# Four small VectorE steps of a query softmax rewritten for GpSimd, the turned halves in a slot of their own, and a new table of order offsets

## The chip, the cores and the metric

The kernel runs on one core of a Trainium2 chip. The metric is the device time of one execution in microseconds (us). Three runs of the kernel before the change took 1722.93, 1723.33 and 1721.21 us, a median of 1722.93. The execution whose profile is read below took 1722.68 us; its span from the first to the last instruction is 1721.0 us, so 1.7 us lie outside the span.

Five engines work side by side: PE (TensorE, matrix products), DVE (VectorE), ACT (ScalarE), POOL (GpSimd) and SP (SyncE, which here only issues DMAs). Each engine takes its instructions in the order in which the program lists them and waits at each for what that instruction needs.

## What is computed

Two attention blocks on 2048 tokens of width 1024 with 32 heads of 32, their outputs side by side. The change touches block B, a linear attention whose feature map is a pair of softmaxes:

```python
def _B_ref(x, wqkv, w_phi, wo):
    q, k, v = ...                                      # x @ wqkv, by heads
    pq = jnp.einsum("bhsd,hdf->bhsf", q, w_phi)
    pk = jnp.einsum("bhsd,hdf->bhsf", k, w_phi)
    phi_q = jnp.concatenate([_softmax(pq, axis=-1), _softmax(-pq, axis=-1)], axis=-1)
    phi_k = jnp.concatenate([_softmax(pk, axis=-1), _softmax(-pk, axis=-1)], axis=-1)
    kv = jnp.einsum("bhsf,bhsd->bhfd", phi_k, v)
    z  = jnp.einsum("bhsf->bhf", phi_k)
    num = jnp.einsum("bhqf,bhfd->bhqd", phi_q, kv)
    den = jnp.einsum("bhqf,bhf->bhq", phi_q, z)[..., None] + 1e-6
    o = num / den
    return ... @ wo
```

Block A is a causal attention over four segments with a running memory, and ends in its own product with an output matrix.

## The kernel before

**Stages.** Times are from the trace. From 0 to about 850 us run 32 units of block A (attention, with B's weights folded and B's tokens prepared between them). From about 850 to 927 us B's first values follow, up to 1189 us the keys and remaining values of B in eight pairs of 128-token tiles, from 1189 to about 1573 us B's queries (the *query stage*), and from 1561 us to the end the output product of block A.

**Products.** Numbers are kept as two float16 halves (a high part and the rest), so a product is three matrix instructions. The large products go by a Strassen scheme over a pair of token tiles: seven half-size products into three PSUM banks X, Y and Z (`strassen`, products at L610), four results out.

**The query stage** runs over 16 token tiles `c`. For each even `c` one Strassen product of 84 instructions gives four results, one for each tile of the pair and each half `hb` of the heads. `expo` takes each result: per-head maximum and minimum (L1264), the two differences into the tile `e` (L1266, L1268), four exponentials (ACT, L1271), the sums of both softmaxes (L1274) and their reciprocals `r` (L1277). Then for each tile and `hb`, a *unit* (32 in all): GpSimd multiplies `e` by the key sums `zb` in two parts (L1579), VectorE sums each part (`dn`, L1582), then four small VectorE instructions make the common factor: `dn*r` (L1585), both halves of it added with 1e-6 (L1587), its reciprocal (L1589), and `r` times that reciprocal times 2^14 (L1590). GpSimd multiplies `e` by `r` (L1592). ACT writes the high half of the result as float16 (L1601), VectorE the rest (L1603), both into a tile `eh`. SP turns `eh` with a transposing DMA into `pt` (L1606). PE multiplies `pt` by the key-value sums `kls` (24 instructions, L1615), ACT and VectorE write both halves of that to `ot` (L1619, L1621), and `project` multiplies `ot` by B's output matrix (48 instructions for a tile, L396) and stores it.

**Buffers.** A buffer with a tag is a ring: a new one takes the place of the one as many back as the ring has places, and its first writer waits for all uses of that older one. `e` and `eh` share the ring "e" of five. For a pair of tiles the program asks for four `e`, then four `eh`, then the next pair's four `e`. So the `eh` of the second unit takes the place of the first `e`, and the first `e` of the next pair that of the fourth `e` of this pair. Slots S0 to S15 are single buffers of [128, 2, 4, 512] float16. The seven forms of the query weights lie in the slots listed in `VS` (S0, S1, S2, S3, S9, S11, S15).

**A's output weights** are also made in the query stage, on ACT and GpSimd (`weights`, in tiles 5, 7, 9, 11): of their seven forms, B11, B21 and T1 are written straight into slots S8, S13 and S12, the other four go over buffers `cs` to DRAM (`wo_d`) and are loaded at tile 14 (L1568) into the first slots of the query weights.

**The order.** The program doesn't fix the order of instructions by hand. Each operation is given to `Graph.op` with an engine, a planned duration, a priority (the stage's number) and what it reads and writes. `Graph.run` walks through a planned time and at each step lets the ready operation with the lowest priority go next on its engine; `lat` and `kb` tell it how long a DMA takes to land. That list is what each engine then runs in order. Operations with the same priority in a row are a *job*; the table `MOVES` adds an offset to the priority of one engine's part of one job. Job numbers 20 to 235 belong to block A and the values, 238 to 284 to the keys, 285 to 390 to the query stage.

Of the kernel before, what the change touches and what calls it, by code (L numbers as in the profile page):

```python
# [18 lines left out]
S = 2048  # L19
# [22 lines left out]
VS = (0, 1, 2, 3, 9, 11, 15)  # L42
# [12 lines left out]
         ((3, 0, "subtract"), 3, 2), ((2, 3, "subtract"), 2, 6))  # L55
EUP = 2.0 ** 15
MOVES = {
# [6 lines left out]
    "DVE": {  # L64
# [4 lines left out]
    "ACT": {  # L69
# [3 lines left out]
    "POOL": {  # L73
        59: 0.5, 67: 5.5, 70: -0.5, 93: -6, 141: 5, 154: -8, 173: 3, 199: 12, 202: -3, 211: -16.5, 234: -5.5, 238: -29.5,
        250: -2, 252: 1.5, 257: 0.5, 312: -11.5, 326: -7},
    "SP": {
        88: 5, 89: 2.5, 107: -2.5, 131: 3, 134: 21.5, 183: 8, 184: -7, 223: 6.5, 226: -9, 238: -37},
}


# [197 lines left out]
SP, PE, ACT, DVE, POOL = "SP", "PE", "ACT", "DVE", "POOL"  # L278
# [3 lines left out]
def tile_kernel(ctx: ExitStack, tc: tile.TileContext, ax, aw, awv, awo, beta, bx, bwqk, bwv, bphi, bwo, out):  # L282
    nc = tc.nc
# [5 lines left out]
    dram = ctx.enter_context(tc.tile_pool(name="scratch", bufs=1, space=DRAM))  # L289
    oa_d = dram.tile([NT, 128, NG, 128], F32, name="oa_d")  # L290
    wf_d = dram.tile([3, 7, 128, 2, 4, 512], F16, name="wf_d")
    xf_d = dram.tile([NT // 2, 128, 7, 2, 4, 128], F16, name="xf_d")
    wo_d = dram.tile([4, 128, 2, 4, 512], F16, name="wo_d")
    bo_d = dram.tile([2, 2, 128, 2, 4, 512], F16, name="bo_d")
    wa_d = dram.tile([NG, 128, 2, 2, NC, 128], F16, name="wa_d")
    wva_d = dram.tile([4, 128, 2, NC, 256], F16, name="wva_d")
# [56 lines left out]
    for t in vfb:  # L353
        nc.gpsimd.memset(t[:, :, 128:132], 1.0)

    G = Graph(pools)
    op = G.op
# [5 lines left out]
       w=[gates], prio=0.2, lat=2.0, kb=16)  # L363
# [919 lines left out]
    def ev(e):  # L1283
        return e().rearrange("p h s d -> p (h s d)")
# [86 lines left out]
    for at_, p in enumerate(SEQ):  # L1371
        P = PB + 2 * at_
# [126 lines left out]
    for n in range(2):  # L1499
        for q in range(2):  # L1500
            op(SP, 0.6, lambda n=n, q=q: nc.sync.dma_start(bo[n][q](), bo_d[n, q]), r=[(bob, (n, q))],
               w=[lanes[q]] + [(bo[n][q], (a, i)) for a in range(2) for i in range(4)], prio=P + 1, lat=1.0, kb=1024)
    wform = {}
    ast = G.buf("b", [128, 16], F32, "ast", 1)

    def blocks(j, prio):
# [15 lines left out]
            op(DVE, 0.1, lambda: nc.vector.tensor_tensor(wsc[:, 2, 1, 0:1], wsc[:, 2, 0, 0:1], osc2[:, 0, 0:1], op=OP.mult),  # L1522
               r=[(wscs, (2, 0)), (oscs, 0)], w=[(wscs, (2, 1))], prio=prio)

    SECOND, wob = ("T2", "T3", "B22", "T4"), G.fixed(wo_d)

    def weights(j, prio):

# [17 lines left out]
    for c in range(NT):  # L1546
# [9 lines left out]
                x = x1 if c == 0 else xkept(c // 2 + 1, XS, P)  # L1556
        ot = G.buf("b", [128, 2112], F16, "ot", 4)
        if c == 2:
            for f, i in (("B11", 8), ("B21", 13), ("T1", 12)):
                wform[f] = G.buf("slot", [128, 2, 4, 512], F16, f"S{i}")  # L1560
        if c in (1, 2, 3, 4):
            sizes_out(c - 1, P + 0.5)
# [1 line left out]
            weights((c - 5) // 2, P + 0.5)  # L1564
        if c == 14:
            for i, f in enumerate(SECOND):
                wform[f] = G.buf("slot", [128, 2, 4, 512], F16, f"S{i}")
                op(SP, 0.6, lambda i=i, f=f: nc.sync.dma_start(wform[f](), wo_d[i]), r=[(wob, i)],  # L1568
                   w=[(wform[f], (a, n)) for a in range(2) for n in range(4)], prio=P + 0.5, lat=1.0, kb=1024)

# [3 lines left out]
        for hb in range(2):  # L1574
            e, r = er[c % 2, hb]
            dn = G.buf("b", [128, 16, 2], F32, "dn", 2)
            for a in range(2):
                h0 = 16 * hb + 8 * a
                op(POOL, 1.35, lambda a=a, h0=h0, e=e: nc.gpsimd.tensor_tensor(  # L1579
                    e()[:, 8 * a:8 * a + 8], e()[:, 8 * a:8 * a + 8], zv()[:, h0:h0 + 8], op=OP.mult),  # L1580
                   r=[zb, r], w=[(e, ("x", a))], prio=P)
                op(DVE, 0.66, lambda a=a, e=e, dn=dn: nc.vector.tensor_reduce(  # L1582
                    dn()[:, 8 * a:8 * a + 8], e()[:, 8 * a:8 * a + 8], axis=AX.X, op=OP.add), r=[(e, ("x", a))], w=[(dn, a)], prio=P)
            d1 = G.buf("b", [128, 16], F32, "d1", 2)
            op(DVE, 0.1, lambda dn=dn, r=r: nc.vector.tensor_tensor(dn(), dn(), r(), op=OP.mult),  # L1585
               r=[dn, r], w=[dn], prio=P)
            op(DVE, 0.1, lambda dn=dn, d1=d1: nc.vector.scalar_tensor_tensor(  # L1587
                d1(), dn()[:, :, 0], 1e-6, dn()[:, :, 1], op0=OP.add, op1=OP.add), r=[dn], w=[d1], prio=P)
            op(DVE, 0.15, lambda d1=d1: nc.vector.reciprocal(d1(), d1()), r=[d1], w=[d1], prio=P)  # L1589
            op(DVE, 0.1, lambda d1=d1, r=r: nc.vector.scalar_tensor_tensor(  # L1590
                r(), r(), 2.0 ** 14, d1()[:, :, None].to_broadcast([128, 16, 2]), op0=OP.mult, op1=OP.mult), r=[d1, r], w=[r], prio=P)
            op(POOL, 1.95, lambda e=e, r=r: nc.gpsimd.tensor_tensor(e(), e(), bc32(r), op=OP.mult),  # L1592
               r=[e, r], w=[e], prio=P)
            pt = G.buf("b", [128, 2, 8, 128], F16, "pt", 3)
            eh = G.buf("b", [128, 16, 2, 32], F32, "e", 5)

            def hv(eh=eh):
                return eh().rearrange("p h s d -> p (h s d)").bitcast(F16).rearrange("p (a n) -> p a n", a=2)

            for q in range(2):  # L1600
                op(ACT, 0.53, lambda q=q, e=e, hv=hv: nc.scalar.activation(  # L1601
                    hv()[:, 0, 512 * q:512 * q + 512], ev(e)[:, 512 * q:512 * q + 512], AF.Copy), r=[e], w=[(eh, (0, q))], prio=P)
                op(DVE, 0.7, lambda q=q, e=e, hv=hv: nc.vector.tensor_tensor(  # L1603
                    hv()[:, 1, 512 * q:512 * q + 512], ev(e)[:, 512 * q:512 * q + 512], hv()[:, 0, 512 * q:512 * q + 512], op=OP.subtract),
                   r=[e, (eh, (0, q))], w=[(eh, (1, q))], prio=P, port=True)
            op(SP, 0.6, lambda pt=pt, hv=hv: nc.sync.dma_start_transpose(  # L1606
                pt().rearrange("p a g t -> p (a g) t"), hv().rearrange("p a n -> p (a n)")),
               r=[(eh, (a, q)) for a in range(2) for q in range(2)], w=[pt], prio=P, lat=2.0, kb=512)
            pn = bank("pv", [128, 4, 128])

            def f(pn=pn, pt=pt, hb=hb):
                for g in range(4):
                    for a, b in ((0, 0), (0, 1), (1, 0)):
                        for k in range(2):
                            nc.tensor.matmul(pn()[64 * k:64 * k + 64, g, :], kls()[:, a, 8 * hb + 2 * g + k, :], pt()[:, b, 2 * g + k, :],  # L1615
                                             start=(a + b == 0), stop=(a == 1), skip_group_check=True)

            op(PE, 0.85, f, r=[(kls, (0, hb)), (kls, (1, hb)), pt], w=[pn], prio=P)
            op(ACT, 0.55, lambda pn=pn, hb=hb, otv=otv: nc.scalar.activation(  # L1619
                otv()[:, 0, 4 * hb:4 * hb + 4, :], pn(), AF.Copy, scale=2.0 ** -15), r=[pn], w=[(ot, (0, hb))], prio=P)  # L1620
            op(DVE, 0.62, lambda pn=pn, hb=hb, otv=otv: nc.vector.scalar_tensor_tensor(  # L1621
                otv()[:, 1, 4 * hb:4 * hb + 4, :], pn(), 2.0 ** -15, otv()[:, 0, 4 * hb:4 * hb + 4, :], op0=OP.mult, op1=OP.subtract),
               r=[pn, (ot, (0, hb))], w=[(ot, (1, hb))], prio=P)
# [117 lines left out]
```

## Time and profile before

| | us |
|---|---|
| median of three runs | 1722.93 |
| the profiled execution | 1722.68 |
| its span | 1721.0 |
| PE busy | 1670.3 (97% of the span) |
| DVE busy | 1408.9 (82%) |
| ACT busy | 1159.6 (67%) |
| POOL busy | 955.2 (56%) |
| mean granted TensorE clock | 0.992 |

How to read it: the profile's page gives busy time by engine and by slices of the span; groups of instructions by line, with busy time, mean duration and the idle time of the engine just before them together with what ended that idle time; and the chain of waits that ended last. "x" is a count. A matrix instruction's duration includes its way through the array, and the next one starts before it ends: busy PE is not PE at its peak, so the prediction counts instructions and multiplies by their spacing. PEclk is the granted share of TensorE's clock. An instruction that is held inside its engine counts as busy, with a longer duration.

### The profile page before, as it was taken

The numbers are of one execution on the slowest core, as the hardware profiler recorded it, in microseconds if no ns is written. First come the engines' busy times: TensorE is split into PE (matmuls) and PEld (weight loads), VectorE is DVE, ScalarE is ACT, GpSimd is POOL, SyncE is SP. The second block draws the span as 40 slices with busy tenths as digits, with TensorE's granted clock in tenths as the row PEclk, the third lists the DMA queues.
The fourth block names the chain that finished last, engine by engine and source line by source line (L and its number), as shares of the span: only waits on it lengthen the run. The fifth ranks groups of instructions, "written<-read, shape, count | busy, mean of one in ns | idle before, by whom it ended". The sixth has DMA issues, their size and how long they took to land.

```text
span 1721.0 us, 38652 instructions
## 1 busy us (share of the span) xinstructions
PE 1670.3 (97%) x14408; PEld 1002.9 (58%) x14408; DVE 1408.9 (82%) x3269; ACT 1159.6 (67%) x2131; POOL 955.2 (56%) x1184
## 2 busy tenths in 40 slices
PE   8999999999999999999999999999799899999999
PEld 6667677676776776677755545455344444444444
DVE  6999999899998767797885889778999999987441
ACT  8788999888888978678854676665445554345331
POOL 3346588653668775756742678645656767440000
PEclk9999999999999999999999999999989999999999
DMA  6556456666666573764467464566456565646311
GB/s 211 162 167 185 155 186 190 216 182 184 196 188 204 148 217 94 203 192 115 150 189 258 148 215 135 177 220 251 156 125 149 127 175 128 196 107 198 121 67 61
DMA packets 260699, 290.37 MB, mean 169 GB/s; under 512 B 138784, under 2 KB 191776, under 8 KB 253984
## 3 DMA queue, kind: packets, MB, share of 16 engines
q1 hardware_dynamic: 260512, 287.91, 55.7%
q8 instruction: 113, 1.85, 0.5%
q14 instruction: 74, 0.61, 0.1%
HBM read 160.12 MB, written 85.00 MB: 142 GB/s over the span
## 4 chain that ended last, share of the span: by engine, by line
PE 45%; DVE 15%; DMA 2%; ACT 2%; issue 1%; POOL 1%; SPq 0%; DVEq 0%; ACTq 0%; POOLq 0%
PE proj L610 14%; PE proj L396 8%; PE proj L1669 5%; PE s L610 3%; PE misc L396 3%; DVE e L1603 3%; PE s L1669 2%; DMA pt<-e 2%; PE misc L610 2%; DVE mx L1264 2%; DVE r L1274 1%; DVE dn L1582 1%; PE pv L1009 1%; PE s L973 1%; PE misc L1669 1%
## 5 line engine op out<-in xcount | busy, mean ns | idle before, releaser
L396 PE MATMUL proj<-S,S 128*128 128x128 f16 (+1 forms) x3072 | 504.6, 300 | 4.8 <-DVE S L431 1.8
L396 PEld LDWEIGHTS <-S 128*128 128x128 f16 x4608 | 329.7, 98 | 150.7 <-issue 9.3
L610 PE MATMUL proj<-S,S 128*128 128x512 f16 x1584 | 368.4, 381 | 8.3 <-ACT cs L616 6.1
L610 PEld LDWEIGHTS <-S 128*128 128x128 f16 x2016 | 191.9, 98 | 226.1 <-issue 12.8
L986 POOL TENSOR_SCALAR_AFFINE_SELECT ph<-ph 128x256 f16<-128x256 f16 (+1 forms) x448 | 194.3, 456 | 165.5 <-DVE ph L980 147.9
L878 DVE CUSTOM_DVE_ANT_0 s<-s,causal 128x256 f32<-128x256 f32 (+3 forms) x512 | 242.9, 508 | 14.1 <-PE s L872 10.8
L980 DVE SCALAR_TENSOR_TENSOR ph<-s,ph 128x512 f16<-128x512 f32 x320 | 211.0, 684 | 51.6 <-ACT ph L979 50.2
L979 ACT ACTIVATE ph<-s 128x512 f16<-128x512 f32 x320 | 191.5, 659 | 0.8
L396 PE MATMUL misc<-S,ot 128*128 128x512 f16 x768 | 172.5, 382 | 1.1 <-ACT ot L1619 1.1
L1271 ACT ACTIVATE e<-e,sk 128x256 f32<-128x256 f32 x256 | 113.8, 497 | 55.3 <-DVE e L1268 46.1
L396 PEld LDWEIGHTS <-ot 128*128 128x128 f16 x768 | 74.2, 98 | 90.8 <-issue 2.2
L1579 POOL TENSOR_TENSOR e<-e,zb 128x512 f32<-128x512 f32 x64 | 86.1, 1369 | 56.5 <-DVE r L1274 45.4
L973 PE MATMUL s<-S 104*128 104x512 f16 (+3 forms) x512 | 114.7, 299 | 0.9 <-DVE mu L951 0.5
L872 PE MATMUL s<-S 96*128 96x512 f16 (+3 forms) x512 | 113.2, 299 | 0.8 <-DVE mt L878 0.4
L977 ACT ACTIVATE s<-s,os 128x512 f32<-128x512 f32 x160 | 106.2, 714 | 9.5 <-PE s L973 6.8
L977 ACT ACTIVATE s<-s,bd 128x512 f32<-128x512 f32 x160 | 106.8, 712 | 5.5 <-PE s L973 4.8
L396 PE MATMUL proj<-wv,S 128*128 128x128 f16 x1536 | 104.9, 219 | 0.1
L1601 ACT ACTIVATE e<-e 128x512 f16<-128x512 f32 x64 | 37.3, 622 | 97.0 <-POOL e L1592 47.5
L1009 PEld LDWEIGHTS <-ph 128*128 128x128 f16 x2560 | 87.3, 96 | 17.7 <-issue 1.4
L1009 PE MATMUL pv<-vl,ph 128*128 128x66 f16 (+1 forms) x2560 | 92.2, 184 | 0.8 <-DVE h L826 0.3
L1274 DVE TENSOR_REDUCE r<-e 128x32 f32<-128x1024 f32 x64 | 76.6, 1207 | 12.5 <-ACT e L1271 12.4
L1592 POOL TENSOR_TENSOR e<-e,r 128x1024 f32<-128x1024 f32 x32 | 64.8, 2029 | 39.6 <-DVE r L1590 35.8
(342 smaller groups left out, 3355.2 us busy)
## 6 DMA issues: line engine op xcount, KB each, us to landing
S<-xf_d SPq DMA_DIRECT2D x126, 256.0 KB
S<-h SPq DMA_DIRECT2D x192, 128.0 KB
S<-wf_d SPq DMA_DIRECT2D x21, 1024.0 KB
st<-bwqk SPq DMA_DIRECT2D x64, 256.0 KB
out<-os SPq DMA_DIRECT2D x40, 256.0 KB
S<-aw SPq DMA_DIRECT2D x16, 512.0 KB
wa_d<-S SPq DMA_DIRECT2D x16, 512.0 KB
wf_d<-fo SPq DMA_DIRECT2D x32, 256.0 KB
```

What stands on the lines that cost most here:

```text
L396: op(PE, dur, lambda c=c, a=a, b=b, lv=lv, rv=rv: nc.tensor.matmul(pv(), lv(), rv(), start=(c == 0 and a + b == 0), stop=(c == n - 1 and a ...
L610: op(PE, 0.215, lambda n=n, a=a, b=b, lv=lv, rv=rv: nc.tensor.matmul(ps(), lv(), rv(), start=(start and n == 0 and a + b == 0), stop=(n == ...
L872: nc.tensor.matmul(ps()[:, o:o + 128 * i + 128], st()[0:96, 0, h, 128 * i:128 * i + 128], st()[0:96, 1, h, 0:128 * i + 128], start=True, s ...
L878: dve(0.12 + 0.00113 * n, lambda h=h, i=i, o=o, n=n: nc.vector.tensor_tensor_reduce(ps()[:, o:o + n], ps()[:, o:o + n], causal[:, 512 - n: ...
L973: nc.tensor.matmul(ps()[:, o:o + n], st()[0:104, 1, h, 128 * j:128 * j + 128], st()[0:104, 0, h, 128 * j:512], start=True, stop=True)
L977: act(0.59, lambda: nc.scalar.activation(ps(), ps(), AF.Exp, bias=0.0, scale=bdv()[:, 3, i2, 0:1]), r=[(bd, i2)], w=[ps])
L979: act(0.5, lambda: nc.scalar.activation(ph()[:, 0], ps(), AF.Copy, scale=2.0 ** 14), r=[ps], w=[(ph, 0)])
L980: dve(0.6, lambda: nc.vector.scalar_tensor_tensor(ph()[:, 1], ps(), 2.0 ** 14, ph()[:, 0], op0=OP.mult, op1=OP.subtract), r=[ps, (ph, 0)], ...
L986: nc.gpsimd.affine_select(pd, pd, pattern=[[0, n], [1, 128]], compare_op=OP.is_ge, fill=0.0, base=0, channel_multiplier=-1)
L1009: nc.tensor.matmul(ps()[:, i, n0:n1], ph()[:, a, o:o + 128], vl()[:, j, h, n0:n1], start=(i == 0 and a == 0), stop=(j == min(i, 2)), skip_ ...
L1271: op(ACT, 0.41, lambda i=i: nc.scalar.activation(e()[:, 4 * i:4 * i + 4], e()[:, 4 * i:4 * i + 4], AF.Exp, bias=0.0, scale=sk()[:, i:i + 1 ...
L1669: op(PE, 0.215, lambda n=n, a=a, b=b: nc.tensor.matmul(ps(), v(a)[:, n, :], wform[w]()[:, b, n, :], start=(start and n == 0 and a + b == 0 ...
```

## The change

1. In each unit of the query stage `dn*r`, the scaling and the product of `r` with the reciprocal move to GpSimd as three instructions (planned at 0.25 us each). The sum of the two halves of `dn` becomes a reduction on VectorE; 1e-6 and the factor 2^14 go into the GpSimd instruction behind it (as 2^-14 ahead of the reciprocal). VectorE keeps the reduction and the reciprocal.
2. `eh` leaves the ring "e". One buffer in slot S13, [128, 2, 2048] float16, holds the halves of both `hb`; each `hb` has its own part of it.
3. Form B21 of A's output weights leaves S13: its halves go over `cs` to DRAM too (`wo_d` has five places), and it is loaded at tile 14. The five loaded forms go into the first five slots of `VS`: S0, S1, S2, S3, S9.
4. The transposing DMA is planned with 2.9 us on SP instead of 0.6, a landing time of 1.2 instead of 2.0 and 64 KB instead of 512 of DMA flow.
5. `MOVES` is replaced as a whole, with entries for all stages (jobs 20 to 363 before, 43 to 384 now).

```diff
 MOVES = {
+    "DVE": {
+        43: -3, 44: -1, 70: 2.5, 85: -19, 88: -3.5, 93: -7.5, 101: -3.5, 103: 7, 106: -22.5, 109: 2.5, 113: -3.5, 114: -9.5,
...
+        222: -14, 229: -1, 238: -62.5, 243: -1.5, 250: -19, 296: -0.5, 307: 2, 308: -40.5, 312: -15.5, 317: -2, 318: -15.5,
+        332: 5, 338: -11.5, 350: -2.5, 358: -1.5, 370: 3, 381: -13.5, 387: -7.5},
...
     "PE": {
-        20: -6.5, 22: -12.5, 76: -7, 79: -15.5, 83: -4, 96: -5, 101: 2, 102: 4, 104: 2, 107: 5.5, 108: 15.5, 113: 1.5,
...
     "SP": {
-        88: 5, 89: 2.5, 107: -2.5, 131: 3, 134: 21.5, 183: 8, 184: -7, 223: 6.5, 226: -9, 238: -37},
+        88: 7, 89: 7, 151: 6.5, 167: 6, 169: 2.5, 199: 9.5, 217: -5, 250: -6, 363: 4.5},
 }
...
-    wo_d = dram.tile([4, 128, 2, 4, 512], F16, name="wo_d")
+    wo_d = dram.tile([5, 128, 2, 4, 512], F16, name="wo_d")
...
+    eh = G.buf("slot", [128, 2, 2048], F16, "S13")
...
-    SECOND, wob = ("T2", "T3", "B22", "T4"), G.fixed(wo_d)
+    SECOND, wob = ("B21", "T2", "T3", "B22", "T4"), G.fixed(wo_d)
...
-            for f, i in (("B11", 8), ("B21", 13), ("T1", 12)):
+            for f, i in (("B11", 8), ("T1", 12)):
...
-                wform[f] = G.buf("slot", [128, 2, 4, 512], F16, f"S{i}")
+                wform[f] = G.buf("slot", [128, 2, 4, 512], F16, f"S{VS[i]}")
...
-            op(DVE, 0.1, lambda dn=dn, r=r: nc.vector.tensor_tensor(dn(), dn(), r(), op=OP.mult),
+            op(POOL, 0.25, lambda dn=dn, r=r: nc.gpsimd.tensor_tensor(dn(), dn(), r(), op=OP.mult),
                r=[dn, r], w=[dn], prio=P)
-            op(DVE, 0.1, lambda dn=dn, d1=d1: nc.vector.scalar_tensor_tensor(
-                d1(), dn()[:, :, 0], 1e-6, dn()[:, :, 1], op0=OP.add, op1=OP.add), r=[dn], w=[d1], prio=P)
+            op(DVE, 0.12, lambda dn=dn, d1=d1: nc.vector.tensor_reduce(d1(), dn(), axis=AX.X, op=OP.add), r=[dn], w=[d1], prio=P)
+            op(POOL, 0.25, lambda d1=d1: nc.gpsimd.tensor_scalar(d1(), d1(), 1e-6, 2.0 ** -14, op0=OP.add, op1=OP.mult), r=[d1], w=[d1], prio=P)
             op(DVE, 0.15, lambda d1=d1: nc.vector.reciprocal(d1(), d1()), r=[d1], w=[d1], prio=P)
-            op(DVE, 0.1, lambda d1=d1, r=r: nc.vector.scalar_tensor_tensor(
-                r(), r(), 2.0 ** 14, d1()[:, :, None].to_broadcast([128, 16, 2]), op0=OP.mult, op1=OP.mult), r=[d1, r], w=[r], prio=P)
+            op(POOL, 0.25, lambda d1=d1, r=r: nc.gpsimd.tensor_tensor(
+                r(), r(), d1()[:, :, None].to_broadcast([128, 16, 2]), op=OP.mult), r=[d1, r], w=[r], prio=P)
...
-            eh = G.buf("b", [128, 16, 2, 32], F32, "e", 5)
-
-            def hv(eh=eh):
-                return eh().rearrange("p h s d -> p (h s d)").bitcast(F16).rearrange("p (a n) -> p a n", a=2)
+            def hv(hb=hb):
+                return eh()[:, hb].rearrange("p (a n) -> p a n", a=2)
...
-            op(SP, 0.6, lambda pt=pt, hv=hv: nc.sync.dma_start_transpose(
+            op(SP, 2.9, lambda pt=pt, hv=hv: nc.sync.dma_start_transpose(
                 pt().rearrange("p a g t -> p (a g) t"), hv().rearrange("p a n -> p (a n)")),
-               r=[(eh, (a, q)) for a in range(2) for q in range(2)], w=[pt], prio=P, lat=2.0, kb=512)
+               r=[(eh, (hb, a, q)) for a in range(2) for q in range(2)], w=[pt], prio=P, lat=1.2, kb=64)
```

The reads and writes of `eh` in L1601 and L1603 name the part (`hb`, ...) in the same way.

More of the change, by code (lines that the diff above doesn't have):

```diff
@@ L57 @@
 MOVES = {
[6 rows of a table removed]
-    "DVE": {
[4 rows of a table removed]
-    "ACT": {
[3 rows of a table removed]
-    "POOL": {
-        59: 0.5, 67: 5.5, 70: -0.5, 93: -6, 141: 5, 154: -8, 173: 3, 199: 12, 202: -3, 211: -16.5, 234: -5.5, 238: -29.5,
-        250: -2, 252: 1.5, 257: 0.5, 312: -11.5, 326: -7},
+    "DVE": {
[4 rows of a table added]
+    "ACT": {
[4 rows of a table added]
+    "POOL": {
[8 rows of a table added]
     "SP": {
-        88: 5, 89: 2.5, 107: -2.5, 131: 3, 134: 21.5, 183: 8, 184: -7, 223: 6.5, 226: -9, 238: -37},
[1 row of a table added]
 }
@@ L1594, in tile_kernel @@
             pt = G.buf("b", [128, 2, 8, 128], F16, "pt", 3)
-            eh = G.buf("b", [128, 16, 2, 32], F32, "e", 5)
-            def hv(eh=eh):
-                return eh().rearrange("p h s d -> p (h s d)").bitcast(F16).rearrange("p (a n) -> p a n", a=2)
+            def hv(hb=hb):
+                return eh()[:, hb].rearrange("p (a n) -> p a n", a=2)
             for q in range(2):
                 op(ACT, 0.53, lambda q=q, e=e, hv=hv: nc.scalar.activation(
-                    hv()[:, 0, 512 * q:512 * q + 512], ev(e)[:, 512 * q:512 * q + 512], AF.Copy), r=[e], w=[(eh, (0, q))], prio=P)
+                    hv()[:, 0, 512 * q:512 * q + 512], ev(e)[:, 512 * q:512 * q + 512], AF.Copy), r=[e], w=[(eh, (hb, 0, q))], prio=P)
                 op(DVE, 0.7, lambda q=q, e=e, hv=hv: nc.vector.tensor_tensor(
                     hv()[:, 1, 512 * q:512 * q + 512], ev(e)[:, 512 * q:512 * q + 512], hv()[:, 0, 512 * q:512 * q + 512], op=OP.subtract),
-                   r=[e, (eh, (0, q))], w=[(eh, (1, q))], prio=P, port=True)
-            op(SP, 0.6, lambda pt=pt, hv=hv: nc.sync.dma_start_transpose(
+                   r=[e, (eh, (hb, 0, q))], w=[(eh, (hb, 1, q))], prio=P, port=True)
+            op(SP, 2.9, lambda pt=pt, hv=hv: nc.sync.dma_start_transpose(
                 pt().rearrange("p a g t -> p (a g) t"), hv().rearrange("p a n -> p (a n)")),
-               r=[(eh, (a, q)) for a in range(2) for q in range(2)], w=[pt], prio=P, lat=2.0, kb=512)
+               r=[(eh, (hb, a, q)) for a in range(2) for q in range(2)], w=[pt], prio=P, lat=1.2, kb=64)
             pn = bank("pv", [128, 4, 128])
```

23 rows, old and new, of the table MOVES are left out of this document.

## The prediction

> **What bounds the kernel now.** I read first where the engines are full, then the query stage by windows, then its instructions by line. The page's slices of 43 us:
>
> ```profile
> PE   8999999999999999999999999999799899999999
> DVE  6999999899998767797885889778999999987441
> PEclk9999999999999999999999999999989999999999
> ```
>
> PE falls below 0.9 in the first slice and in slices 29 and 32 (1205 to 1248 and 1334 to 1377 us), the clock in slice 30, and DVE stands at nine tenths from slice 29 to slice 35 without a break. That is the query stage, so I cut it into windows:
>
> ```profile
> core 0: us, PE busy (x) PEld busy (x) DVE busy (x) ACT busy (x) POOL busy (x), PEclk, DMA share, GB/s
> 100.00:1189.00 1089.00, 1081.63 (x10627) 703.21 (x10625) 917.91 (x2382) 849.90 (x1573) 692.82 (x954) 1.00 0.59 182
> 1205.00:1549.00 344.00, 313.51 (x2086) 150.80 (x2085) 321.80 (x516) 159.52 (x311) 214.00 (x147) 0.97 0.56 145
> 1226.00:1272.00 46.00, 31.33 (x210) 14.66 (x208) 43.10 (x71) 16.88 (x35) 25.31 (x18) 0.81 0.36 77
> 1272.00:1561.00 289.00, 274.00 (x1814) 129.88 (x1813) 262.19 (x410) 132.70 (x257) 177.71 (x121) 0.99 0.60 151
> ```
>
> DVE is busy for 321.8 of 344 us (94%), POOL for 214.0. From 100 to 1189 us PE lacks only 1089 - 1081.6 = 7.4 us. PE's own busy time flatters it, so I count its instructions. The spacing at full clock comes from block A's output product, the counts from the windows of L610 (Strassen), L396 (project) and L1615 (pv), in this order:
>
> ```profile
> 1584.64 2.75 PE L1669 MATMUL s<-S,pt 128*128 128x512 f16 x12
> 1587.23 2.75 PE L1669 MATMUL proj<-S,h 128*128 128x512 f16 x12
> ...
> 1476.96 0.86 PE L1615 MATMUL pv<-pt,kls 128*64 128x128 f16 x24
> ...
> 1226.00:1272.00 46.00, 23.17 (x92) 8.97 (x89) 0.81 0.36 77
> 1272.00:1561.00 289.00, 99.21 (x444) 42.56 (x444) 0.99 0.60 151
> ...
> 1226.00:1272.00 46.00, 4.89 (x22) 2.25 (x23) 0.81 0.36 77
> 1272.00:1561.00 289.00, 156.58 (x698) 67.20 (x697) 0.99 0.60 151
> ...
> 1226.00:1272.00 46.00, 4.17 (x96) 3.44 (x96) 0.81 0.36 77
> 1272.00:1561.00 289.00, 24.10 (x672) 20.19 (x672) 0.99 0.60 151
> ```
>
> Twelve large instructions start 2.59 us apart: 0.216 us each; a pv one costs 0.86/24 = 0.036. From 1226 to 1272 PE had (92+22) x 0.216 + 96 x 0.036 = 28.1 us of work: 18 us lost in this *filling* of the stage. From 1272 to 1561 it had 1142 x 0.216 + 672 x 0.036 = 270.9 us, so 18 us were lost in the *steady* part. These 36 us are all that this change can win in its own stage; behind 1561 us PE is full.
>
> Two things hold PE there. One is DVE's work. The other is the ring "e":
>
> ```profile
> 1292.87 0.69 DVE L1603 TENSOR_TENSOR e<-e 128x512 f16<-128x512 f32 x1 [0.26 <-ACT e L1601]
> 1293.48 0.68 DVE L1266 TENSOR_TENSOR e<-proj,mx 128x512 f32<-128x512 f32 x1
> ```
>
> The first difference of the next pair starts only where the last unit of the pair before is being converted, as the ring demands (its fourth `e` must be free). Until then the Strassen results stay in their banks.
>
> **The change part by part.**
>
> *Small steps.* DVE's groups between 1205 and 1549 us, then the shortest, median and longest of three of them:
>
> ```profile
> L1603 DVE TENSOR_TENSOR e<-e 128x512 f16<-128x512 f32 x64 | 75.9, 1221 | 12.4 <-ACT e L1601 12.2
> L1582 DVE TENSOR_REDUCE dn<-e 128x16 f32<-128x512 f32 x64 | 41.7, 665 | 0.1
> L1274 DVE TENSOR_REDUCE r<-e 128x32 f32<-128x1024 f32 x32 | 38.3, 1204 | 1.2 <-ACT e L1271 1.1
> L1585 DVE TENSOR_TENSOR dn<-dn,r 128x32 f32<-128x32 f32 x32 | 21.6, 676 | 0.3
> L1587 DVE SCALAR_TENSOR_TENSOR d<-dn 128x16 f32<-128x16 f32 x32 | 12.0, 385 | 0.2
> L1590 DVE SCALAR_TENSOR_TENSOR r<-r,d 128x32 f32<-128x32 f32 x32 | 10.1, 326 | 0.2
> ...
> L1582 DVE TENSOR_REDUCE dn<-e x64: 622/673/687, 1224.8 to 1540.8; 128x16 f32<-128x512 f32 x64
> L1585 DVE TENSOR_TENSOR dn<-dn,r x32: 121/533/1584, 1226.8 to 1541.5; 128x32 f32<-128x32 f32 x32
> L1603 DVE TENSOR_TENSOR e<-e x64: 674/947/2446, 1239.6 to 1548.6; 128x512 f16<-128x512 f32 x64
> ```
>
> The three instructions that leave cost 21.6 + 12.0 + 10.1 = 43.7 us. Most of that is being held: L1585 can run in 0.12 us and takes 0.68 on average. What holds it is seen here:
>
> ```profile
> 1369.11 1.91 POOL L1592 TENSOR_TENSOR e<-e,r 128x1024 f32<-128x1024 f32 x1 [1.40 <-DVE r L1590]
> 1369.16 1.91 DVE L1590 SCALAR_TENSOR_TENSOR r<-r,d 128x32 f32<-128x32 f32 x1
> ```
>
> A DVE instruction with two SBUF inputs, started beside a POOL one, ends with it. Reductions (L1582, 622 to 687 ns) are not held. So the new reduction of 32 elements costs, from L1274 and L1582, 1.05 ns an element and a fixed 0.13: 0.16 us, or 5.1 us for 32; if it were held like L1585, 21.6. I take 5.1. DVE: -43.7 + 5.1 = -38.6.
>
> Some holding comes back: L1603 loses 1221 - 674 = 0.55 us on 64 instructions, 35 us, while POOL is busy for 62% of the stage; with POOL at some 75% (below) that is 42, so +7. DVE nets -32 us, 1.0 a unit. The least is the bare run time, 3 x 0.12 x 32 = 11.5, less 5.1: -6, all holding having moved to L1603. I keep -32, since an instruction that isn't there can't be held.
>
> POOL gains 96 instructions; the nearest rows are
>
> ```profile
> L1030 POOL TENSOR_TENSOR rd<-rd,sc 128x16 f32<-128x16 f32 x32 | 8.2, 257 | 15.8 <-DVE rd L1029 13.2 <-DVE pst L534 1.0 <-DVE bd L742 0.9
> L1276 POOL TENSOR_SCALAR r<-r 128x32 f32<-128x32 f32 x32 | 10.0, 315 | 43.2 <-DVE r L1274 37.2 <-DVE big L551 3.1 <-DVE wsc L411 2.8
> L952 POOL TENSOR_TENSOR mem<-mem,mu 128x132 f32<-128x132 f32 x24 | 11.6, 484 | 24.0 <-DVE mu L951 13.0 <-PE misc L925 10.8
> ```
>
> Between 0.26 and 0.48 us each; by size (32 elements, 2 ns an element above L1030) 0.29, 0.32 and 0.29, so 0.9 a unit and 29 us for the stage (25 to 46). POOL then has 243 of some 330 us: 74%, not full, and hidden.
>
> The work passes between POOL and DVE two times more in each direction in a unit. DVE's waits for POOL are bounded below by L1582: 64 hand-overs, 0.1 us idle in all, since the planner lists other DVE work in between. I take near 0; the other end is the slow rival.
>
> *Own slot for the halves.* `eh` of one `hb` is written again a tile later, two units or about 21 us; the old one must have been turned, which takes SP
>
> ```profile
> L1606 SPq DMA_TRANSPOSE pt<-e x32: 1322/2164/4082, 1242.6 to 1551.9; - x32
> ```
>
> so no wait. With five places for `e` alone, the next pair's first `e` is free at once and the second when the first unit is converted, so L1266 may run up to three units earlier. It adds no work; its worth lies between 0 and the 18 us of filling, and I count it with DVE's relief.
>
> *B21 over DRAM.* Four stores of 256 KB and one more load beside these four:
>
> ```profile
> S<-wo_d SPq DMA_DIRECT2D x4, 1024.0 KB
> 1481.45 8.09 SPq L1568 DMA_DIRECT2D S<-wo_d  x4
> ```
>
> The loads leave by 1489.5 and their first use is behind 1561. One more megabyte at the 151 GB/s of the window is 7 us, landing well before; S0 is free first, its product being the first of the last Strassen. Cost 0; without that cover 7 us in front of block A's second product.
>
> *Planned time of the turning DMAs.* Nothing on the chip costs less. SP really spends 1.3 to 4.1 us on each, planned at 0.6, so the loads and stores queued behind came up to 3.5 us late in the plan's eyes. It removes a misfit of the order; I count 0, at worst a few us of either sign, held in the range.
>
> *The table.* From 100 to 1189 us it can win at most the 7.4 us above and lose as much again without a new mechanism; I take 0.
>
> *Sum.* Steady part: DVE needed 94% of it; with 32/344 = 9% less it has a tenth to spare, and PE becomes the limit. I take two thirds of the 18 us, 12, as jitter and the end of the stage stay. Filling: DVE was busy for 43.1 of 46 us, with four units before the first products flow; 4 x 1.0 = 4 us less, 0 to 18 by the ring. Together -16, a touch less for the longer path of the first unit: -15. 1722.7 - 15 = **1708 us**; the profiled run lies 0.25 us below the median, which changes nothing.
>
> **The rivals.**
>
> *The holding only moves* (DVE -6 us). For it: L1603's median of 947 against 674. Against it: the held steps stand between reductions that are not held, as L1585 does between two L1582, so what follows them often runs free. Then the DVE-bound stage shortens by 6 to 7: 1716 us.
>
> *The filling closes too.* PE waits there for the first turned tile, and the clock falls:
>
> ```profile
> 1247.06 1.49 PE L1615 MATMUL pv<-pt,kls 128*64 128x128 f16 x24 [11.04 <-DMA pt<-e]
> 1251.61 5.28 PE L610 MATMUL proj<-S,S 128*128 128x512 f16 x12 [3.06 <-ACT cs L616]
> ```
>
> Twelve products took 5.28 us instead of 2.59: half speed after 11.04 us of idling. If the ring lets PE work through, most of the 36 us comes back: 1722.7 - 33 = 1690. Against it: the first unit's chain is as long as before, with more hand-overs. The Trainium skill (TensorE: Matmul & The Clock Gate, Part 1) says that an idle window of about 3.4 us halves the clock until a busy one has passed. By that rule the gap must shrink below a third before the clock's part is saved; the trace agrees as far as the half speed goes.
>
> *Slower: POOL's turn-taking.* POOL takes its list in order, and three of its instructions in a unit now wait for DVE where one did. Its waits in the stage:
>
> ```profile
> POOL e L1579 <- DVE r L1274: 45.4, 9, 11.4
> POOL e L1592 <- DVE r L1590: 35.8, 25, 4.3
> ```
>
> Busy 214 + 29 and these 81 make 324 of 344. With 64 new waits POOL bounds the stage once each lasts over 20/64 = 0.3 us. At 0.6 it is 362: +18, 1741 us; at the row's 35.8/25 = 1.4 it would be 1790. Against it: the 81 us are mostly POOL with nothing to do while DVE is full, and shrink as DVE gets faster. The Trainium skill (GPSIMD Engine Reference, 4.1 Engine selection) gives small elementwise work to VectorE, with GpSimd some two times slower on two inputs. The trace agrees (0.26 us in L1030 against 0.12 in L1585 unheld), but by that rule POOL's part would be 3 x 0.24 x 32 = 23 us, which changes no chance while POOL is not full.
>
> *The table costs more than the stage wins*: a stall before 1189 us. PE is at 99% there with little to show for it; 1728.
>
> **How the numbers follow.** Forecast 1708 (its own range 1697 to 1714): 0.50. Holding moves, 1716: 0.18. Filling closes, 1690: 0.10. POOL's turns, 1741: 0.14. Table, 1728: 0.08. A measurement of this kernel tells 0.2%, 3.4 us, from no change. Faster than 1719.5: 0.50 + 0.10 + 0.15 of the second = 0.75. Within: the rest of the second and half of the table's, 0.07. Slower: 0.14 + 0.04 = 0.18. The range 1694 to 1730 leaves out about 0.08 below and 0.12 above.
>
> **What would show it.** Right: DVE below 295 us busy in the query stage, a `dn` reduction near 0.16 us that is never held, L1266 of the next pair well ahead of the last L1603, PE's lost time in the steady part under 8 us. Wrong: L1603's mean above 1.5 us (holding moved); DVE idle before the small reduction or reciprocal, released by POOL, of 10 us and more (turn-taking); PE's lack before 1189 us above 12 us (table).

## The result and the profile after

The changed kernel takes 1705.67 us (median of four runs, 1704.54 to 1706.96); the kernel before took 1722.73 beside it. The ratio is 0.990, with an interval of 0.9885 to 0.992: 17 us less, where 1708 was forecast.

The slices of the page after, of 43 us each, for the engines that were shown before:

```profile
PE   8999999999999999999999999999999999999999
DVE  6889999899888878888885778877998887996441
PEclk9999999999999999999999999999999999999999
```

PE has no dent left in the query stage, and the clock is not lowered there. Then the stages, before and after, cut at the same events: the first Strassen product of the queries (1189 us before, 1196 after) and the first product of block A's output (1561 and 1546). The first fence is the kernel before, the second the changed one; its last three rows are the filling and the steady part, set 7 us later than before, and a window that begins 16 us behind the stage's start and ends 12 us ahead of its end, as 1205 to 1549 us did in the prediction.

```profile
1189.00:1561.00 372.00, 341.51 (x2278) 164.55 (x2277) 340.03 (x547) 173.66 (x338) 222.62 (x155) 0.97 0.59 153
```

```profile
core 0: us, PE busy (x) PEld busy (x) DVE busy (x) ACT busy (x) POOL busy (x), PEclk, DMA share, GB/s
100.00:1189.00 1089.00, 1075.80 (x10584) 699.99 (x10582) 915.32 (x2374) 846.13 (x1566) 688.21 (x951) 1.00 0.59 182
...
1196.00:1546.00 350.00, 338.00 (x2292) 163.25 (x2291) 305.75 (x492) 177.26 (x344) 245.88 (x251) 1.00 0.64 166
1233.00:1279.00 46.00, 42.04 (x294) 19.95 (x293) 43.62 (x79) 24.86 (x49) 35.31 (x40) 1.00 0.46 98
1279.00:1546.00 267.00, 261.10 (x1745) 123.88 (x1744) 227.38 (x351) 131.57 (x252) 193.25 (x197) 1.00 0.68 169
1212.00:1534.00 322.00, 310.00 (x2103) 149.74 (x2102) 285.52 (x460) 162.00 (x313) 237.85 (x243) 1.00 0.64 163
```

The query stage is 22 us shorter (350 against 372), but it begins some 7 us later: up to 1189 us PE now lacks 1089 - 1075.8 = 13.2 us instead of 7.4. VectorE is busy in the stage for 305.8 us instead of 340.0, GpSimd for 245.9 instead of 222.6. In the filling VectorE is as busy as before (43.6 of 46 us against 43.1): there it does other work, not less.

PE's lost time is counted as in the prediction, from the windows of L611 (Strassen), L397 (project) and L1615 (pv) of the changed kernel, in this order:

```profile
1233.00:1279.00 46.00, 27.43 (x123) 11.68 (x122) 1.00 0.46 98
1279.00:1546.00 267.00, 96.04 (x424) 40.23 (x422) 1.00 0.68 169
...
1233.00:1279.00 46.00, 11.27 (x49) 4.53 (x49) 1.00 0.46 98
1279.00:1546.00 267.00, 149.53 (x671) 64.65 (x671) 1.00 0.68 169
...
1233.00:1279.00 46.00, 4.30 (x120) 3.60 (x120) 1.00 0.46 98
1279.00:1546.00 267.00, 23.24 (x648) 18.88 (x648) 1.00 0.68 169
```

Filling: 172 x 0.216 + 120 x 0.036 = 41.5 of 46 us, 4.5 lost instead of 18. Steady part: 1095 x 0.216 + 648 x 0.036 = 259.8 of 267, 7 lost instead of 18. These two add up to some 24 us, the stage is 22 us shorter: its first 37 us hold 10 large products fewer than before (129 against 139 of L611 and L610).

VectorE's groups of the stage, the spread of two of them, and GpSimd's groups:

```profile
L1603 DVE TENSOR_TENSOR S<-e,S 128x512 f16<-128x512 f32 x64 | 69.9, 1128 | 9.7 <-ACT S L1601 9.7
L1584 DVE TENSOR_REDUCE dn<-e 128x16 f32<-128x512 f32 x64 | 42.0, 670 | 2.3 <-POOL e L1581 2.1
L1591 DVE RECIPROCAL d<-d 128x16 f32<-128x16 f32 x32 | 7.8, 245 | 3.6 <-POOL d L1590 3.3
L1589 DVE TENSOR_REDUCE d<-dn 128x16 f32<-128x32 f32 x32 | 5.2, 174 | 2.5 <-POOL dn L1587 2.1 <-POOL r L1592 0.4
...
L1589 DVE TENSOR_REDUCE d<-dn x32: 127/176/189, 1235.4 to 1526.8; 128x16 f32<-128x32 f32 x32
L1603 DVE TENSOR_TENSOR S<-e,S x64: 627/761/2397, 1243.9 to 1535.2; 128x512 f16<-128x512 f32 x64
```

```profile
L1581 POOL TENSOR_TENSOR e<-e,zb 128x512 f32<-128x512 f32 x64 | 85.8, 1359 | 26.9 <-DVE r L1275 25.7 <-ACT zb L1452 0.6
L1594 POOL TENSOR_TENSOR e<-e,r 128x1024 f32<-128x1024 f32 x32 | 64.5, 2017 | 1.2
L1592 POOL TENSOR_TENSOR r<-r,d 128x32 f32<-128x32 f32 x32 | 11.8, 371 | 6.2 <-DVE d L1591 6.1
...
L1587 POOL TENSOR_TENSOR dn<-dn,r 128x32 f32<-128x32 f32 x32 | 9.8, 306 | 20.9 <-DVE dn L1584 20.5
...
L1590 POOL TENSOR_SCALAR d<-d 128x16 f32<-128x16 f32 x32 | 8.4, 264 | 14.9 <-DVE d L1589 12.8
```

The new reduction takes 0.17 us and never more than 0.19: it is not held beside GpSimd. The three GpSimd steps take 9.8 + 8.4 + 11.8 = 30 us. VectorE's idle time put down to GpSimd before L1584, L1589 and L1591 is 2.1 + 2.5 + 3.3 = 7.9 us. And the order on VectorE at the first change of pairs:

```profile
1240.56 0.68 DVE L1267 TENSOR_TENSOR e<-proj,mx 128x512 f32<-128x512 f32 x1
...
1256.52 1.29 DVE L1603 TENSOR_TENSOR S<-e,S 128x512 f16<-128x512 f32 x2
```

The next pair's first difference runs 16 us ahead of this pair's last conversion. Before, the ring let it begin only behind the third unit's conversions, while the last unit was being converted:

```profile
1247.81 1.52 DVE L1603 TENSOR_TENSOR e<-e 128x512 f16<-128x512 f32 x2 [0.76 <-ACT e L1601]
...
1249.85 0.68 DVE L1266 TENSOR_TENSOR e<-proj,mx 128x512 f32<-128x512 f32 x1
...
1251.77 1.28 DVE L1603 TENSOR_TENSOR e<-e 128x512 f16<-128x512 f32 x2
```

It must be the third, because the Strassen scheme gives the four results in the order (0,0), (1,1), (0,1), (1,0) of tile and `hb`, so that the fourth `e` is that of the third unit.

### The profile page after: what moved, and what is told of

The parts are those of the page before. It is cut to its first block, busy times and chain, and to the rows that moved or that the text cites. A ratio compares the mean times of both kernels' runs of the same rounds, so it can differ in the third digit from the quotient of the medians.

```text
span 1705.2 us, 38661 instructions
## 1 busy us (share of the span) xinstructions
PE 1667.3 (98%) x14408; PEld 1001.9 (59%) x14408; DVE 1372.7 (80%) x3205; ACT 1159.1 (68%) x2131; POOL 976.8 (57%) x1280
## 4 chain that ended last, share of the span: by engine, by line
PE 54%; DVE 15%; ACT 4%; POOL 2%; DMA 2%; issue 2%; SPq 0%; ACTq 0%; DVEq 0%; POOLq 0%
PE proj L611 13%; PE proj L397 11%; PE misc L397 6%; PE proj L1669 5%; PE s L611 3%; PE s L1669 2%; DVE s L879 2%; PE s L974 2%; PE pv L1010 2%; PE s L873 2%; PE misc L611 2%; DVE S L1603 1%; DVE mx L1265 1%; PE misc L1669 1%; DVE ph L981 1%
## 5 line engine op out<-in xcount | busy, mean ns | idle before, releaser
L397 PE MATMUL proj<-S,S 128*128 128x128 f16 (+1 forms) x3072 | 507.9, 300 | 3.9 <-DVE S L432 1.4
L397 PEld LDWEIGHTS <-S 128*128 128x128 f16 x4608 | 329.4, 98 | 145.5 <-issue 8.0
L611 PE MATMUL proj<-S,S 128*128 128x512 f16 x1584 | 365.2, 379 | 3.6 <-ACT cs L617 3.6
L611 PEld LDWEIGHTS <-S 128*128 128x128 f16 x2016 | 192.2, 98 | 220.9 <-issue 5.0
L879 DVE CUSTOM_DVE_ANT_0 s<-s,causal 128x512 f32<-128x512 f32 (+3 forms) x512 | 243.6, 507 | 9.7 <-PE s L873 5.5
L397 PE MATMUL misc<-S,ot 128*128 128x512 f16 x768 | 171.3, 379 | 0.7 <-ACT ot L1619 0.6
L397 PEld LDWEIGHTS <-ot 128*128 128x128 f16 x768 | 73.9, 98 | 89.5 <-DVE ot L1621 0.9
L397 PE MATMUL proj<-wv,S 128*128 128x128 f16 x1536 | 102.6, 219 | 0.0
L1581 POOL TENSOR_TENSOR e<-e,zb 128x512 f32<-128x512 f32 x64 | 85.8, 1359 | 26.9 <-DVE r L1275 25.7
L1603 DVE TENSOR_TENSOR S<-e,S 128x512 f16<-128x512 f32 x64 | 69.9, 1128 | 9.7 <-ACT S L1601 9.7
L879 DVE DVE_READ_ACCUMULATOR2_ANT mt<- 128x1 f32 x512 | 72.3, 141 | 0.0
```

The source lines that it names most:

```text
L397: op(PE, dur, lambda c=c, a=a, b=b, lv=lv, rv=rv: nc.tensor.matmul(pv(), lv(), rv(), start=(c == 0 and a + b == 0), stop=(c == n - 1 and a ...
L611: op(PE, 0.215, lambda n=n, a=a, b=b, lv=lv, rv=rv: nc.tensor.matmul(ps(), lv(), rv(), start=(start and n == 0 and a + b == 0), stop=(n == ...
L879: dve(0.12 + 0.00113 * n, lambda h=h, i=i, o=o, n=n: nc.vector.tensor_tensor_reduce(ps()[:, o:o + n], ps()[:, o:o + n], causal[:, 512 - n: ...
```

## The experiments

The change has five parts that act together on one planned order, so there are two kinds of runs. Three keep an order word for word and take instructions out of it or put some in; in the others one part is undone, or done alone, and the order is planned anew. Medians are given with the ratio to the kernel before of the same runs; PE's lost time is counted as above. "Filling" is the 46 us from 37 us after the stage's first Strassen product.

### VectorE's time by itself, the order kept

**Before, the three steps left out.** The emptied operations stay in the plan:

```diff
-            op(DVE, 0.1, lambda dn=dn, r=r: nc.vector.tensor_tensor(dn(), dn(), r(), op=OP.mult),
+            op(DVE, 0.1, lambda: None,
...
-            op(DVE, 0.1, lambda dn=dn, d1=d1: nc.vector.scalar_tensor_tensor(
-                d1(), dn()[:, :, 0], 1e-6, dn()[:, :, 1], op0=OP.add, op1=OP.add), r=[dn], w=[d1], prio=P)
-            op(DVE, 0.15, lambda d1=d1: nc.vector.reciprocal(d1(), d1()), r=[d1], w=[d1], prio=P)
+            op(DVE, 0.1, lambda: None, r=[dn], w=[d1], prio=P)
+            op(DVE, 0.15, lambda dn=dn, d1=d1: nc.vector.reciprocal(d1(), dn()[:, :, 0]), r=[d1], w=[d1], prio=P)
...
+            op(DVE, 0.1, lambda: None, r=[d1, r], w=[r], prio=P)
```

> The kernel before in its own order, with the three small VectorE instructions of each unit (dn*r, the sum with 1e-6, r times the reciprocal) left out, so that the query's denominator is left out of the result; nothing is added on GpSimd and the halves stay in the ring. VectorE loses 44 us of busy time in the query stage. Theory, that the ring and not VectorE's work held the filling: only the steady part wins, 1711 to 1717 us. Rival, that VectorE's time is all that bounds the stage: 1698 to 1706 us. Second rival, that the holding by GpSimd moves to the next instruction: 1718 to 1722, with L1603 above 1.5 us on average.

1701.35 us, 0.988 (0.9864 to 0.9897): the rival's range. The stage from 1189 to 1541 us and L1603 in it, now at line 1601:

```profile
1189.00:1541.00 352.00, 338.86 (x2279) 163.62 (x2278) 302.23 (x449) 173.97 (x336) 220.60 (x155) 0.98 0.62 163
```

```profile
L1601 DVE TENSOR_TENSOR e<-e 128x512 f16<-128x512 f32 x64 | 77.9, 1254 | 15.8 <-ACT e L1599 15.8
```

The stage is 20 us shorter with the ring and the order of before. PE still loses 14 us in the filling and under 2 behind it: these steps cost the whole of the loss in the steady part, and none that shows in the filling. The run takes away more than VectorE's time, though. Without the steps GpSimd need not wait for the common factor either: its idle time before the product of `e` with `r` (L1592, here L1590) fell from 35.8 to 4.9 us. So it prices the steps with their wait; the next run prices the time alone. The conversions are held about as long as before (1254 ns against 1221), so the time that the steps were held didn't move to them.

**Changed kernel, VectorE's load put back.**

```diff
+    dump = const.tile([128, 8], F32, name="dump")
...
-            op(DVE, 0.15, lambda d1=d1: nc.vector.reciprocal(d1(), d1()), r=[d1], w=[d1], prio=P)
+            def inverse(d1=d1):
+                nc.vector.reciprocal(d1(), d1())
+                nc.vector.tensor_reduce(dump, ident[:, None, 0:104].to_broadcast([128, 8, 104]), axis=AX.X, op=OP.add)
+
+            op(DVE, 0.15, inverse, r=[d1], w=[d1], prio=P)
```

> The changed kernel in its own order with a reduction of 832 elements of a constant added on VectorE behind each unit's reciprocal (about 1.0 us, 32 in all), which is what the change took off VectorE net. Theory A, that VectorE's time bounds the steady part: 1716 to 1726 us (VectorE is back above 94% busy there). Theory B, that there is slack on VectorE now and the order and the slot carry the gain: at most 1710.

1721.64 us, 0.9996 (0.9985 to 1.0007): theory A. VectorE's list has 32 instructions more, those of ACT, GpSimd and SyncE are unchanged; the added reduction and the stage:

```profile
L1594 DVE TENSOR_REDUCE dump<-ident 128x8 f32<-128x832 f32 x32 | 30.8, 963 | 0.0
```

```profile
1192.00:1560.00 368.00, 344.92 (x2292) 165.43 (x2290) 334.28 (x523) 176.86 (x344) 242.18 (x251) 0.98 0.56 156
```

31 us of VectorE work cost 16 us of time, with the slot, the table and the GpSimd steps in place. The stage is 368 us long again. By the count of PE's work the steady part loses 20 us instead of 7, the filling 8 instead of 4.5. The added reduction stands behind the reciprocal that GpSimd waits for, so the unit's own chain is not what it lengthens.

**Changed kernel, two GpSimd steps left out.** `dn*r` and the step with 1e-6 are emptied in the same way.

> The changed kernel in its own order with two of the three GpSimd steps of each unit left out (dn*r, and 1e-6 with 2^-14, so the softmax's own sums and that scale are left out of the denominator); the reduction, the reciprocal and r times it stay. GpSimd loses 64 instructions, some 18 us, and two hand-overs in a unit. Theory, that GpSimd's steps are hidden: 1702 to 1707 us. Rival, GpSimd's turn-taking costs time that another mechanism outweighed: below 1700.

1706.09 us, 0.9906 (0.9889 to 0.9922): the same as the changed kernel. 64 GpSimd instructions and their hand-overs cost nothing there; the turn-taking of these two steps is not what bounds.

### One part alone, on the old table

**The small steps alone** on the kernel before (the GpSimd and VectorE lines of the change's diff, nothing else).

> The kernel before with the small steps on GpSimd alone: old table, halves in the ring, B21 in S13, SyncE's time as before. The order is planned anew. Theory A, VectorE's relief works in the steady part without the slot (leaving the steps out won 20 us with no work added on GpSimd): 1702 to 1712 us, filling still above 12 us lost. Theory B, the steps need the slot or new offsets (with the halves in the ring and the new table it took 1725.7): 1718 and more.

1703.41 us, 0.9889 (0.9874 to 0.9904): theory A, with the halves in the ring. The windows are the whole stage, the filling and the rest, and L1603:

```profile
1191.00:1544.00 353.00, 338.27 (x2280) 164.18 (x2279) 294.55 (x486) 175.71 (x340) 242.71 (x251) 0.99 0.62 163
1228.00:1274.00 46.00, 34.56 (x249) 17.02 (x248) 41.52 (x70) 18.12 (x37) 33.38 (x37) 0.89 0.46 101
1274.00:1544.00 270.00, 267.53 (x1777) 127.14 (x1775) 218.29 (x350) 133.51 (x257) 189.53 (x197) 1.00 0.64 159
```

```profile
L1603 DVE TENSOR_TENSOR e<-e 128x512 f16<-128x512 f32 x64 | 65.4, 1055 | 16.4 <-ACT e L1601 15.9
```

This one part, a score of lines, is as fast as the whole change. The filling is as bad as before (14 us lost, the clock lowered to 0.89); the steady part loses 3.

**The own slot alone**, with B21 over DRAM.

```diff
...
+    eh = G.buf("slot", [128, 2, 2048], F16, "S13")
...
-    SECOND, wob = ("T2", "T3", "B22", "T4"), G.fixed(wo_d)
+    SECOND, wob = ("B21", "T2", "T3", "B22", "T4"), G.fixed(wo_d)
...
```

> The kernel before with the own slot for the halves and B21 over DRAM alone: old table, small steps on VectorE, SyncE's time as before. Theory A, the slot closes the filling only (18 us lost before, 12 with the whole structure and the old table), VectorE still bounds the steady part: 1714 to 1720. Theory B, no worth without VectorE's relief: 1721 to 1726. Rival to both, the slot is the main gain: below 1712.

1720.36 us, 0.9986 (0.9977 to 0.9996): between theory A's upper edge and B: 2 us, by the interval 1 to 4. In its filling PE lost 18 us as before; the slot alone does not close it.

### One part undone, on the new table

> The changed kernel with the halves back in the ring e of five places (as before the change); the steps on GpSimd, form B21 over DRAM, SyncE's planned time and the new table stay. The order is planned anew. Theory A: the own slot is what let the filling close (PE lost 18 us there before, 5 after), so the filling loses 12 us and more again: 1714 to 1720 us. Theory B: VectorE's relief with the new order closes it and the ring is worth little: 1703 to 1709.

1725.65 us, 1.0012 (1.0 to 1.0025), past theory A's range. The filling and the rest:

```profile
1232.00:1278.00 46.00, 36.10 (x236) 17.80 (x235) 40.96 (x70) 20.85 (x40) 30.76 (x34) 0.85 0.34 74
1278.00:1575.00 297.00, 281.67 (x1850) 134.03 (x1849) 235.28 (x376) 142.68 (x269) 192.47 (x203) 0.98 0.64 166
```

With the ring the filling loses 13 us again: on this table the slot is what closes it. But VectorE is busy for 235 of 297 us behind it and PE still lacks 18 there, 11 of them between 1535 and 1560 us, where pv (here L1616) sat idle 10.7 us for the transposing DMA into pt: PE had run 78 instructions of `project` in one go until 1539 us and, but for one pv, had nothing left when the next transposes went out at 1544. It is an order whose offsets were not made for the ring. The old table with the ring (the steps alone) took 1703. So 20 us here are not the price of the ring.

> The changed kernel with the small steps on VectorE as before; own slot, B21 over DRAM, SyncE's planned time and the new table stay. The order is planned anew. Theory A (leaving the steps out of the old order won 20 us): VectorE bounds the steady part again, whose loss of PE time goes from 8 back to 15 us and more: 1714 to 1722 us. Theory B, that the slot and the order made the gain: 1703 to 1709.

1756.62 us, 1.0195 (1.0168 to 1.0221), far past theory A. VectorE's load came back (334 us busy in the stage), and behind the filling PE lost 50 us. 26 of them lie between 1559 and 1595 us, 23.6 of these with pv (L1615) idle for the same kind of DMA. The DMA is only the end of that wait:

```profile
1552.96 15.07 PE L397 MATMUL misc<-S,ot 128*128 128x512 f16 x69
1567.86 0.38 PE L611 MATMUL proj<-S,S 128*128 128x512 f16 x1
1591.85 1.49 PE L1615 MATMUL pv<-pt,kls 128*64 128x128 f16 x24 [23.62 <-DMA pt<-S]
```

The last instruction of the queries' last Strassen product is listed behind 69 instructions of `project`. VectorE sat idle for 13.9 us until its result came, and then the whole chain of the last units ran with PE empty. So this too is an order that fits badly, and the run doesn't price the steps.

> The changed kernel with SyncE's planned time of the transposing DMAs as before (0.6 us, landing 2.0, 512 KB of flow). Only the order is planned anew. Theory: the plan's misfit is worth a few us at most: 1703 to 1710. Rival, that it is what brings the loads behind the transposes in time: 1712 and more, with PE waiting for DMAs in the query stage.

1718.8 us, 0.9978 (0.9966 to 0.9989): the rival's range. Undoing numbers that change nothing on the chip cost 13 us, 10 of them lost on PE between 1515 and 1555 us, by the count of its work. PE's groups there, of this kernel (the last column is the idle time before them and what ended it):

```profile
L397 PE MATMUL misc<-S,ot 128*128 128x512 f16 x120 | 28.6, 397 | 0.0
L1615 PE MATMUL pv<-pt,kls 128*64 128x128 f16 x120 | 4.9, 239 | 7.3 <-DMA pt<-S 7.3
```

The last heads' turned halves land late, as in the two runs above; the changed kernel's pv does not wait there. Whether the true time of SyncE matters or only its fit with the table is what the next pair tells.

### The table

**The whole structure on the old table**, with both planned times of SyncE:

> The changed kernel with the whole old table. Theory: the moved steps and the separate slot make the gain in the query stage (22 us between its first Strassen product and block A's output product) and the new table adds little to it, while the early loss goes: 1695 to 1708 us. Rival, that the gain needs offsets searched for the new work: 1715 us and more, with time lost on PE in the query stage again above 25 us.

1708.53 us, 0.9921 (0.9906 to 0.9936), half a microsecond above the theory's range. PE loses 12 us in the filling and 11 behind it: with the relief and the slot, but without the new table, the filling is not closed.

> The moved steps and the own slot with the whole old table (1708.5 us with the new planned time of SyncE) and SyncE's planned time as before. Theory A, that the offsets have to fit the planned times and a misfit costs whichever way (with the new table the old time cost 13 us): here the old time fits the old table no worse, 1703 to 1713. Theory B, that the true time on SyncE is what orders the queue right: 1716 and more.

1701.68 us, 0.988 (0.9865 to 0.9895): a microsecond below theory A's range, and far from B. The planned time nearer to the chip's gains 13 us on the new table and loses 7 on the old one. It is no gain by itself; that each table's offsets are fitted to what the plan assumed is the reading of these four runs.

**Old offsets for the early jobs in the changed kernel, and new ones in the kernel before:**

```diff
-MOVES = { ... the new table ... }
+MOVES = { ... the old table's jobs below 237, the new table's from 237 on ... }
```

> The changed kernel, with the old table's offsets for jobs below 237 (block A and the values) and the new table's from there on. Theory: the new table lost some 7 us before the query stage (its first Strassen product starts at 1195.8 us instead of 1189.0) and the order there depends on nothing else of the change, so the query stage should start at 1189 (plus or minus 2) and the whole take 1698.5 us (1696 to 1701). Rival: the later start comes from elsewhere, or what the early stages save is waited for again in the query stage: 1704 to 1707.

1698.55 us, 0.9863 (0.9848 to 0.9878): the theory. The stage starts at 1186 us and is as long as in the changed kernel:

```profile
100.00:1186.00 1086.00, 1078.44 (x10597) 701.26 (x10596) 916.28 (x2370) 846.14 (x1566) 692.38 (x953) 1.00 0.60 184
1186.00:1536.00 350.00, 338.65 (x2295) 163.55 (x2294) 305.85 (x492) 176.96 (x344) 245.49 (x251) 1.00 0.64 166
```

It is 7 us faster than the change and 23 faster than the kernel before beside it, the fastest of all runs.

> The kernel before, with the new table's offsets for jobs below 237 and its own from there on; nothing else of the change. Theory: the early offsets alone cost some 7 us: 1729.5 us (1727 to 1732). Rival, that they cost nothing by themselves: 1721 to 1725.

1721.35 us, 0.9999 (0.999 to 1.0009): the rival. The query stage begins later here too, at 1194 us, but takes 364 us instead of 372:

```profile
1194.00:1558.00 364.00, 339.98 (x2250) 162.84 (x2248) 332.19 (x547) 174.19 (x340) 218.34 (x155) 0.97 0.58 150
```

VectorE is busy there for 332 us instead of 340, and PE loses 11 us in the steady part instead of 18. VectorE's list in the stage came out in another order, and what the early jobs lost was made up. Why is not settled by these runs. The seven profiles with the new early offsets start the stage between 1192.1 and 1195.8 us, the seven with the old ones between 1186.5 and 1191.6: about 4.5 us apart on average, less than the single pair of profiles above says.

## Why the prediction was right

The main mechanism held. The number came within 3 us partly by luck: the filling won 9.5 us more than its term, and some 7 were lost ahead of the stage, where the sum had nothing.

- **What bounds.** VectorE in the steady part of the query stage: shown by leaving its steps out in the old order (-20 us, together with GpSimd's wait for them) and by putting 31 us of other work back in the new one (+16).
- **The steps, VectorE.** Forecast -32 us of busy time, measured 340.0 - 305.8 = -34 in the stage, and 285.5 us in the window for which under 295 was the sign. The new reduction was put at 0.16 us and takes 0.17. The +7 for more holding of L1603 had the wrong sign: 75.9 us became 69.9, though GpSimd is busier; the last section has the reason. So the lines that were named won 43.7 - 5.2 + 6.0 = 44.5 us, and that -34 came out near -32 is chance: some 10 us are other work in the stage, such as the output halves of block A that now fall into it (L432, 2.2 us before as L431 and 6.8 now), and neighbouring instructions whose durations overlap. The rival in which the holding only moves is out.
- **The steps, GpSimd.** Forecast 29 us and hidden; 30, and hidden (two steps less change nothing). VectorE waits 7.9 us for it, 5.8 of them before the small reduction and the reciprocal, not 0: small, and under the 10 that were to count against the step. The slow rival is out: GpSimd's waits before L1581 and L1594 fell from 81.2 to about 26 us while the new ones came to some 39.
- **Steady part.** Forecast 12 of 18 us, measured 11; with the steps alone it was 15.
- **Filling: the step that was mis-sized.** Forecast 4 of 18 us, measured 13.5. The prediction named the ring as what could be worth up to 18 and then counted only VectorE's relief, 4 us less to do there; VectorE is as busy there as before. Relief alone leaves 14 us lost, the slot alone 18, both on the old table 12 (10 with the old planned time of SyncE), and all of it with the new table 4.5. On the new table 13 are lost with the ring back and 12 with the steps back on VectorE. It takes both, and an order that uses them. The rival in which the filling closes had the place right; the clock's dip went with it, as it named.
- **Table: the other one.** Forecast 0, measured some 7 us lost ahead of the stage by the pair of profiles, and PE's lack before 1189 us went over the 12 us that were to show it. Taking the old offsets for those jobs gave 7.1 us back. In the kernel before, the same offsets cost nothing in the end.
- **SyncE's planned time** was put at 0 and a few us of either sign; it was -13 and +7, depending on the table. B21's detour cost nothing that shows: from block A's first product to the end it takes 159.5 us, and 159.6 before.

So 13.5 + 11, some 24 us by the count (22 by the stage's length), were won and some 7 lost ahead of it, where 16 and 0 were forecast.

## What to carry to other kernels

Where one engine is full in one stage, small instructions moved off it pay by what they really take there, held time included, and the trace of before gives that; leaving them out of an unchanged order prices the move before it is built. A change to a planned order should be tried part by part on the old and on the new offsets: here one part was worth the whole, and the early half of the new table cost the changed kernel 7 us. An undone part on a table that was fitted without it measures the misfit as well as the part.

## What the runs showed of the hardware that was not expected

A VectorE instruction with two SBUF inputs and 32 elements can take as long as the GpSimd instruction beside it (1.91 us in the trace of before), while reductions of 32 and of 512 elements were not held in the changed kernel (at most 0.19 and 0.69 us).

How long a conversion (L1603) is held can be read off the traces. One from the trace of before, with the GpSimd instruction that runs when it starts:

```profile
1371.21 1.91 POOL L1592 TENSOR_TENSOR e<-e,r 128x1024 f32<-128x1024 f32 x1 [0.19 <-DVE r L1590]
```

```profile
1371.59 2.08 DVE L1603 TENSOR_TENSOR e<-e 128x512 f16<-128x512 f32 x1
```

GpSimd ends at 1373.12 us and the conversion at 1373.67, 0.55 us later. Of the 64 conversions of that trace, 35 end 0.545 to 0.551 us behind the GpSimd instruction during which they started; 27 started while GpSimd ran nothing and took 0.67 to 0.69 us; the other two were not held. In the changed kernel 41 of 64 end 0.54 to 0.62 us behind the GpSimd instruction that ran when they started.

So a conversion that starts during a GpSimd instruction is late by about what is left of it. Averaged over those conversions that was 1.1 us before, 0.8 in the changed kernel and 0.7 with the steps alone; in these two, 6 and 15 of them started during one of the new small steps. So the mean of all 64 fell from 1221 to 1128 and 1055 ns, though GpSimd's share rose: the share does not set how long they are held, which is what the prediction's +7 was scaled by.
